# Packed attention and a SoLU layer on one core: v of three batches without zero rows, two banks for its weighted halves, a split last copy and a new order

## Chip, core and metric

The kernel runs on one core of a Trainium2 chip. Its engines work side by side: TensorE (PE in the profile) multiplies matrices, with the weight loads shown as PEld; VectorE (DVE), ScalarE (ACT) and GpSimd (POOL) work on vectors; SyncE (SP) issues the DMA transfers. Each engine executes its own list of instructions in order, and semaphores make one wait for another. The metric is the device time of the program in microseconds, and a change is judged by the median of several executions.

## The reference

Two stages follow each other. The first is attention over packed queries, for 8 batches of 8 heads with 576 tokens and 64 dimensions: 32 packed queries p look at all keys, and then all queries look at the 32 packed rows. The second is a layer over the 4608 tokens of 512 values, with 1024 hidden values and 64-bit weights.

```python
def sm_attn(qq, kk, vv):                      # scale = 1/8
    s = scale * np.matmul(qq, kk.transpose(0, 1, 3, 2))
    s = s - np.max(s, axis=-1, keepdims=True)
    a = np.exp(s)
    a = a / (np.sum(a, axis=-1, keepdims=True) + 1e-09)
    return np.matmul(a, vv)
p_packed = sm_attn(p, k, v)
out = sm_attn(q, p_packed, p_packed)          # -> x, (4608, 512)
...
h = x @ w_in
e = np.exp(h - np.max(h, axis=-1, keepdims=True))
solu = h * e / (np.sum(e, axis=-1, keepdims=True) + 1e-09)
mu = np.mean(solu, axis=-1, keepdims=True)
var = np.mean((solu - mu) ** 2, axis=-1, keepdims=True)
out = ((solu - mu) / np.sqrt(var + 1e-06) * g_ln) @ w_out
```

## The kernel before

The work is cut into named steps. A step carries a batch (`s10/3`), a tile of 128 tokens (`m1-12`, of 36) or the letter w for the weights (`wb0/w`). Functions register each step with what it needs and which buffers it takes and gives back; the long string `ORDER` lists all steps, and each engine gets its instructions in that order. A suffix names the engine of a step (`:v` VectorE, `:p` GpSimd, `:a` ScalarE) or the first PSUM bank that it writes (`:0` to `:7`, of eight). So an instruction that waits holds up all that stands behind it on its engine.

**Attention, batch b.** `lk0`, `lk1` (L411), `lq0`, `lq1` (L416) and `lv` (L420) load halves of k and q, and v. The packed scores come in two halves `s10`, `s11` (L436, TensorE, f32); `mx` takes their row maximum (L440, VectorE), `mb` the bias, `ex` the exponential on ScalarE, `ri` adds the small guard to the sums (L461 where GpSimd does it), `rs` inverts them (L465). For batches 0 to 2 `tp0` to `tp2` transpose the exponentials on TensorE (L474) and `tc0` to `tc2` copy them to `e1T` (L148); for later batches `eh`, `el`, `et`, `ea` do this with a transposing DMA. `av` (L504) weights v: 40 matmuls into one bank, both halves of the heads side by side. `pp` scales the result (L144 or L142), `pe` takes a peak, `pt` (L520), `pc`, `pk`, `un`, `uq` transpose it and find its scale (`unit`). Then the second attention: `sx0`, `sx1` (L538, TensorE), `sb` (L560), `sm` (L563), `su`, `se`, `ss` (L572), `si`, `sr` (L583), `sn` (L586), `at` (L627, a transpose), `ah` and `al` (L639): its weights as two f16 parts. Only batch 0 does these in two halves (`ss0`, `ss1`). For the layer, `z0`, `z1` (L604) multiply the packed rows with w_in, and `zh`, `zl` (L622) store the product as two f16 parts.

**Token tiles.** `m1` (L723) gives the hidden values h in two banks; `nm` (L729) is the row maximum, `nb` the bias, `bd` (L740 and L742) a bound and the row's scale `s_row`; `ex` (L747) the exponential, `u` (L752) the product e * s_row * h, and only with `u` are the banks of `m1` free again. `yh`, `yl` (L763) split it in f16 parts, `tr` (L767) transposes them by DMA into `yT`; `mu`, `sq` (L771), `ca` (L775 and L776) and `cr` (L781, L782) give the output's factor; `m2a`, `m2b` (L789) multiply with w_out, `ev` scales the result into the output buffer `o_sb` (L142 or L144), and `st` (L796) stores it. Tiles don't come in the order of their numbers: the last to be worked on is tile 31.

**Weights.** The 64-bit floats are read as pairs of 32-bit words and converted on the chip: `lw0` to `lw3` load w_in, `lW0` to `lW3` w_out (L167); `wa` (L182, ScalarE) and `wl` (L188 on VectorE, L142 on ScalarE) take upper words and last bits, `wm` joins them (L199, VectorE, the full width of 1024), `wp` sums squares on TensorE (L207). For w_in, `wb0` takes the peak (L211), `wb1` spreads it (L214) and `wb` makes a power of two, the scale that `un/0` needs; `zw`, `zy` make f16 parts `w_hi`, `w_lo` for later batches. For w_out, `pw0`, `pw1`, `pw` do the same (L291 to L299), `cs` sums columns (L316), `cv` scales the sum, `ct` centres (L323), and `ch` (L148), `cl` (L329) make the f16 parts `wch`, `wcl` that `m2` reads. `hw` are fillers: two matmuls on ones whose result nobody reads (L240).

Buffers: two each of k, q, v, of the output, of `yhl` and `yT`. Part of the weights is loaded into the buffers of k, q, v and z.

## Time and profile before

| | |
|---|---|
| time, median of 3 | 372.27 us (371.93 to 373.23) |
| the profiled execution | 372.9 us, its span 371.1 us |
| mean granted clock of TensorE | 0.991 |
| busy share: TensorE, weight loads | 96%, 45% |
| busy share: VectorE, ScalarE, GpSimd | 75%, 56%, 58% |
| moved by DMA | 70.57 MB, 190 GB/s in the mean |

The span runs from the first to the last instruction; 1.8 us of the execution lie around it. TensorE's busy share is 90% or more in 34 of the 40 equal slices of the span, and below 80% in the first four and the last. VectorE is busy for 80% or more in slices 3 to 8, where the weights are converted and the first tiles come, and less from there on. The DMA engines are full in slices 2 to 5 (422 to 425 GB/s). The profile names a group of instructions by line, engine and operation, with the tile it writes and those it reads; "busy" of TensorE is counted with pipelined matmuls, so that a row of 16 matmuls can be shorter than the sum of its parts.

### The profile page before, as it was taken

The page shows a single profiled execution, that of the slowest core. Times are in us where ns is not written, and L with a number is a line of the kernel's source. Part 1 is how long each engine was busy: PE and PEld are TensorE (multiplying, and loading weights), DVE is VectorE, ACT ScalarE, POOL GpSimd, SP SyncE. Part 2 cuts the span into 40 slices and gives each one's busy share as a digit, 9 for nine tenths or more (in the row PEclk, how much of TensorE's full clock was granted, in tenths as well). Part 3 has the DMA queues.
Part 4 walks back from the last instruction along what each step waited for, and adds up shares of the span by engine and source line. Part 5 has one row for each costly group of instructions (what it writes and reads, how often), then busy time and mean ns, then how long its engine had stood idle before and what let it go on. Part 6 is the DMA issues. An engine that isn't in the chain of part 4 may idle for free.

```text
span 371.1 us, 7650 instructions
## 1 busy us (share of the span) xinstructions
PE 354.9 (96%) x3027; PEld 165.9 (45%) x3027; DVE 278.9 (75%) x421; ACT 209.1 (56%) x357; POOL 214.7 (58%) x304
## 2 busy tenths in 40 slices
PE   6757998999999999999999999999999999999997
PEld 5323554344444444454445445444444444444443
DVE  2388899979898779688788998666795696751820
ACT  3559389876957477364454673362645344641341
POOL 1036769999987755298536573457733674256330
PEclk9898999999999999999999999999999999999999
DMA  7999993599698775959887655135546332351661
GB/s 284 425 422 419 425 382 68 126 266 284 229 191 325 227 171 157 153 150 258 156 212 171 198 115 124 44 97 150 148 115 164 92 113 59 113 141 54 148 170 58
DMA packets 99349, 70.57 MB, mean 190 GB/s; under 512 B 88048, under 2 KB 88048, under 8 KB 97776
## 3 DMA queue, kind: packets, MB, share of 16 engines
q1 hardware_dynamic: 99312, 70.07, 64.8%
q8 instruction: 24, 0.39, 0.4%
q14 instruction: 13, 0.11, 0.1%
HBM read 38.80 MB, written 9.44 MB: 130 GB/s over the span
## 4 chain that ended last, share of the span: by engine, by line
PE 83%; DVE 7%; DMA 6%; POOL 3%; issue 1%; ACT 0%; SPq 0%; POOLq 0%
PE pa L789 41%; PE ps L723 23%; PE ps L789 8%; DMA qT<-in_q_dram 4%; PE ps L604 3%; PE ps L538 2%; PE pa L316 1%; PE pa L504 1%; DMA zh<-in_moe_w_in_dram 1%; POOL wcl L329 1%; PE ps L436 1%; DVE u L752 1%; DVE zl L622 1%; DVE nm L729 1%; DVE yT L323 1%; POOL s L586 1%
## 5 line engine op out<-in xcount | busy, mean ns | idle before, releaser
L789 PE MATMUL pa<-wch,yT 128*128 128x512 f16 x480 | 149.5, 379 | 0.8 <-ACT yhl L148 0.8
L789 PEld LDWEIGHTS <-yT 128*128 128x128 f16 x864 | 83.2, 98 | 104.5 <-issue 4.8
L789 PE MATMUL pa<-wcl,yT 128*128 128x512 f16 x240 | 91.0, 379 | 0.0
L729 DVE TENSOR_REDUCE nm<-ps 128x1 f32<-128x1024 f32 x36 | 43.9, 1220 | 29.1 <-PE ps L723 28.9
L763 POOL TENSOR_TENSOR yhl<-u,yhl 128x1024 f16<-128x1024 f32 x23 | 51.2, 2227 | 21.2 <-ACT yhl L148 9.8
L747 ACT ACTIVATE e<-ps,bias,unit 128x1024 f32<-128x1024 f32 x36 | 43.3, 1202 | 35.4 <-DVE bias L144 28.5
L723 PE MATMUL ps<-zh,a2h 128*128 128x512 f16 (+1 forms) x160 | 54.8, 380 | 0.1
L752 DVE SCALAR_TENSOR_TENSOR u<-e,s_row,ps 128x1024 f32<-128x1024 f32 x36 | 45.6, 1267 | 12.2 <-ACT e L747 9.6
L723 PE MATMUL ps<-zh,a2l 128*128 128x512 f16 (+1 forms) x160 | 54.6, 379 | 0.0
L723 PE MATMUL ps<-zl,a2h 128*128 128x512 f16 (+1 forms) x160 | 54.6, 379 | 0.0
L771 ACT ACTIVATE e<-u,negmu 128x1024 f32<-128x1024 f32 x36 | 41.1, 1143 | 8.0 <-DVE negmu L144 7.8
L723 PEld LDWEIGHTS <-a2h 128*128 128x128 f16 (+1 forms) x320 | 27.7, 100 | 33.9 <-issue 3.1
L740 POOL TENSOR_SCALAR bound<-nm,unit 128x1 f32<-128x1 f32 x22 | 18.9, 859 | 27.1 <-DVE nm L729 27.0
L789 PE MATMUL ps<-wch,yT 128*128 128x512 f16 x96 | 30.2, 379 | 0.0
L142 ACT ACTIVATE o_sb<-pa,c_row 128x512 f32<-128x512 f32 x22 | 14.9, 684 | 25.9 <-POOL c_row L782 9.2
L148 ACT CAST yhl<-u 128x1024 f16<-128x1024 f32 x20 | 20.7, 1041 | 15.3 <-DVE u L752 13.0
L781 POOL TENSOR_SCALAR c_row<-sq,k_out,s_eps 128x1 f32<-128x1 f32 x36 | 14.8, 411 | 20.1 <-ACT e L771 19.4
L782 POOL TENSOR_TENSOR c_row<-c_row,neg_half 128x1 f32<-128x1 f32 x36 | 22.3, 619 | 3.0
L775 POOL TENSOR_SCALAR s_eps<-se,s_row 128x1 f32<-128x1 f32 x36 | 14.5, 402 | 15.3 <-ACT e L747 12.2
L723 PEld LDWEIGHTS <-a2l 128*128 128x128 f16 (+1 forms) x160 | 14.3, 100 | 16.8
L763 DVE TENSOR_TENSOR yhl<-u,yhl 128x1024 f16<-128x1024 f32 x13 | 17.6, 1354 | 2.3 <-ACT yhl L148 2.2
L789 PE MATMUL ps<-wcl,yT 128*128 128x512 f16 x48 | 18.2, 379 | 0.0
...
## 6 DMA issues: line engine op xcount, KB each, us to landing
...
```

What stands on the lines that cost most here:

```text
L142: nc.scalar.activation(out, in_, AF.Copy, scale=scale)
L148: nc.scalar.copy(out, in_)
L723: nc.tensor.matmul(h[rows, 512 * n:512 * n + 512], lhsT=lhsT, rhs=z[:, r, 512 * n:512 * n + 512], start=t == 0, stop=t == end)
L729: nc.vector.tensor_reduce(out=nm, in_=st['h'], axis=AX.X, op=ALU.max, negate=True)
L740: eng.tensor_scalar(out=bound, in0=st['nm'], scalar1=st['nm'], scalar2=st['unit'][:, 2:3], op0=ALU.mult, op1=ALU.max)
L747: nc.scalar.activation(st['e'], st['h'], AF.Exp, bias=st['bias'], scale=st['unit'][:, 1:2], accum_out=st['se'])
L752: nc.vector.scalar_tensor_tensor(out=st['u'], in0=st['e'], scalar=st['s_row'], in1=st['h'], op0=ALU.mult, op1=ALU.mult, accum_out=st['su'])
L763: engines[on(f'yl-{i}', 'v')].tensor_tensor(out=st['y'][:, 1], in0=st['u'], in1=st['y'][:, 0], op=ALU.subtract)
L771: nc.scalar.activation(st['e'], st['u'], AF.Square, bias=st['negmu'], accum_out=st['sq'])
L781: nc.gpsimd.tensor_scalar(out=c_row, in0=st['sq'], scalar1=k_out[:, 0:1], scalar2=s_eps, op0=ALU.mult, op1=ALU.add)
L782: nc.gpsimd.tensor_tensor(out=c_row, in0=c_row, in1=neg_half, op=ALU.pow)
L789: nc.tensor.matmul(st['po'], lhsT=st['yT'][:, a, c], rhs=w[:, c], start=c == 0 and t == 0, stop=c == NFC - 1 and t == 2)
```

## The change

Four things change.

- **v.** For batches 0 to 2 (`NARROW`) v is laid out as nine blocks of 128 rows instead of ten, without the 64 zero rows that filled up each half of the heads. `load_v` is shorter by a tenth there, and `av` uses 64 rows of the middle block for each half. The two halves go to a bank each, so that `av` takes a pair of banks for these batches; it still has 40 matmuls. The second half runs its blocks from the last to the first.
- **The last tile's scaled copy.** Where the tile's index is 35, `output` scales the left 256 columns on ScalarE and the right 256 on VectorE.
- **The order.** `ORDER` is another list throughout, with other engines for many steps. Ahead of the first token tile: `lw1` is loaded ahead of `lk1/1`, and `lw3` behind `lq1/0`; `wl0` and `wl2` go to GpSimd (from VectorE and ScalarE); `at0/0` stands behind `wb0`; fillers are `hw8`, `hw47`, `hw44`, `hw32`, `hw25`, `hw45`, `hw39`, `hw21`, where they were `hw1`, `hw25`, `hw9`, `hw10`, `hw29`, `hw2`. Later, `m1-3` stands ahead of `m1-2`, and `cl3` goes to GpSimd, `yl-3` to VectorE. Both lists end with tile 31.
- **The rest** of the steps is the same, but for the fillers: ten pairs of matmuls in all, where there were nine.

```diff
@@ -20,6 +20,7 @@
 Z_TOP = 14
 A_TOP = 15
 Z16 = 2
+NARROW = 3
 E16 = 3
 E_TOP = 15
 LIFT = 0.6931471805599453 * E_TOP
@@ -27,69 +28,69 @@
 Z_W = 2.0 ** 13
 W_HOME = 'zh zl zh zl kT qT v zh'.split()
 ORDER = '''
-lg/w hw1/w:6 lw0/w hw25/w:7 gx/w wa0/w wl0/w:v wm0/w lw2/w wa2/w wl2/w:a lk0/0 hw9/w:6 s10/0:0 mx0/0 lk1/0 s11/0:2
...
-sq-35 cr-35 ev-35:a ev-32:v st-32 hw33/w:7 hw27/w:7 st-35 hw31/w:7 ca-31 cr-31 ev-31:a st-31
+lg/w gx/w hw8/w:6 lw0/w wa0/w lw2/w wl2/w:p lk0/0 lk1/0 lk0/1 s10/0:0 s11/0:2 mx0/0 mb0/0:a ex0/0 mx1/0 mb1/0:v ex1/0
...
+ev-34:v st-34 hw2/w:7 mu-31:a hw26/w:7 sq-33 cr-33 ev-33:a sq-31 cr-31 ev-31:a st-33 zz/6 st-31
 '''
 
 @with_exitstack
@@ -417,7 +418,9 @@
 
         def load_v():
             st['v'] = raws.tile([P, H * HALF + H * J], F32, name='v', bufs=2)
-            nc.sync.dma_start(st['v'], v[b])
+            wide = H * HALF + H * J * (b >= NARROW)
+            at = b * H * HALF + max(0, b - NARROW) * H * J
+            nc.sync.dma_start(st['v'][:, :wide], v[:, at:at + wide])
 
         def banks(t):
             return (t[:, :512], t[:, 512:])
@@ -494,19 +497,25 @@
             st['e1T'] = att.tile([P, 2 * S], F32, name='e1T')
             by('ea', '').tensor_tensor(out=st['e1T'], in0=st['eT'][:, 0], in1=st['eT'][:, 1], op=ALU.add)
 
+        def halved(t):
+            return (t[:, :D], t[:, D:2 * D])
+
         def av():
-            pav = st['pav'] = one()
+            narrow = b < NARROW
+            st['pav'] = [x[:, :D] for x in banks(two())] if narrow else halved(one())
             e1T, v = (groups(st['e1T']), st['v'].rearrange('p (n g d) -> p n g d', g=G, d=D))
             odd = 2 * S // P // 2
             for r in range(2):
-                for x in range(odd + 1):
+                turn = [(odd * r + x, odd * r + x + r * (not narrow)) for x in range(odd + 1)]
+                for c, n in turn[::-1] if narrow and r else turn:
+                    rows = slice(LEFT * r, LEFT * r + LEFT) if narrow and c == odd else slice(0, P)
                     for g in range(G):
-                        nc.tensor.matmul(pav[32 * g:32 * g + 32, r * D:(r + 1) * D], lhsT=e1T[:, odd * r + x, 32 * g:32 * g + 32], rhs=v[:, (odd + 1) * r + x, g], start=x == 0, stop=x == odd)
+                        nc.tensor.matmul(st['pav'][r][32 * g:32 * g + 32], lhsT=e1T[rows, c, 32 * g:32 * g + 32], rhs=v[rows, n, g], start=c == (2 * odd if narrow and r else odd * r), stop=c == (odd if narrow or r == 0 else 2 * odd))
 
         def pp_rows():
             pp = st['pp'] = att.tile([P, 2, 2, D], F32, name='pp')
             for r in range(2):
-                src = st['pav'][:, r * D:(r + 1) * D].unsqueeze(1).broadcast_to([P, 2, D])
+                src = st['pav'][r].unsqueeze(1).broadcast_to([P, 2, D])
                 scaled(on(f'pp/{b}', 'v'), pp[:, r], src, st['rs'][:, r:r + 1])
 
         def row_peak():
@@ -658,7 +667,7 @@
             at('et', e_swap, after=['el'], takes='eT', gives='eh@eh')
             at('ea', e_join, after=['et'], takes='e1T', gives='eT@et')
         turned = [f'tc{i}' for i in range(3)] if b < E16 else ['ea']
-        at('av', av, after=turned + ['lv'], takes='bank', gives=f'e1T@{turned[0]} v@lv')
+        at('av', av, after=turned + ['lv'], takes='bank bank' if b < NARROW else 'bank', gives=f'e1T@{turned[0]} v@lv')
         at('pp', pp_rows, after=['av', 'rs'], takes='pp', gives='bank@av')
         at('pe', row_peak, after=['pp'])
         at('pt', pp_turn, after=['pp'], takes='bank')
@@ -790,7 +799,11 @@
 
         def output():
             st['o'] = mlp.tile([P, DM], F32, name='o_sb', bufs=2)
-            scaled(on(f'ev-{i}', 'a'), st['o'], st['po'], st['c'])
+            if i == B * S // P - 1:
+                for eng, cols in (('a', slice(0, DM // 2)), ('v', slice(DM // 2, DM))):
+                    scaled(eng, st['o'][:, cols], st['po'][:, cols], st['c'])
+            else:
+                scaled(on(f'ev-{i}', 'a'), st['o'], st['po'], st['c'])
 
         def store():
             nc.sync.dma_start(out[row:row + P, :], st['o'])
@@ -876,9 +889,11 @@
                 a = a.reshape(8, 128, 2304)
         elif name == 'v':
             a = a.reshape(8, 4, 2, 576, 64).transpose(0, 2, 3, 1, 4).reshape(8, 2, 576, 256)
-            a = _np.pad(a, ((0, 0), (0, 0), (0, 64), (0, 0)))
+            narrow = a[:NARROW].reshape(NARROW, 9, 128, 256)
+            a = _np.pad(a[NARROW:], ((0, 0), (0, 0), (0, 64), (0, 0)))
             a[:, 1] = _np.roll(a[:, 1], 64, axis=1)
-            a = a.reshape(8, 10, 128, 256).transpose(0, 2, 1, 3).reshape(8, 128, 2560)
+            a = a.reshape(8 - NARROW, 10, 128, 256)
+            a = _np.concatenate([x.transpose(1, 0, 2).reshape(128, -1) for x in [*narrow, *a]], axis=1)
         elif name == 'moe_g_ln':
             a = a.reshape(8, 128).transpose(1, 0)
         a = _np.ascontiguousarray(a)
```

SyncE, the first loads, from v of batch 0 on. Before (L411 loads k, L416 q, L420 v; `zl_206`, `zl_208`, `kT_210` are w_in's second and fourth quarter and w_out's first):

```order
L420 DMA v_181<-in_v_dram 128x2560
L411 DMA kT_179<-in_k_dram 128x1152
L416 DMA qT_195<-in_q_dram 128x1152 x2
L167 DMA zl_206<-in_moe_w_in_dram 128x2048
L167 DMA zl_208<-in_moe_w_in_dram 128x2048
L167 DMA kT_210<-in_moe_w_out_dram 128x2x1024
```

The same stretch after, where the lines count a little higher (`zl_176` and `zl_318` are now w_in's second and fourth quarter, `kT_142` is the second half of batch 1's k):

```order
L423 DMA v_174<-in_v_dram 128x2304
L168 DMA zl_176<-in_moe_w_in_dram 128x2048
L417 DMA qT_262<-in_q_dram 128x1152
L412 DMA kT_142<-in_k_dram 128x1152
L417 DMA qT_262<-in_q_dram 128x1152
L168 DMA zl_318<-in_moe_w_in_dram 128x2048
L168 DMA kT_322<-in_moe_w_out_dram 128x2x1024
```

v is narrower, a quarter of w_in has moved ahead of k's second half, and that half now stands between the halves of q.

VectorE, around the peak of the weights (`wb0`, L211). Before (L188 `wl3`, L199 `wm3`, L627 `at0/0`, L225 the first instruction of `wb`):

```order
L188 TENSOR_SCALAR u_372<-zl_208 128x1024
L583 RECIPROCAL sm_296<-sm_296 128x18
L199 SCALAR_TENSOR_TENSOR w_in_sb_82<-e_341,u_372 128x1024
L627 STREAM_TRANSPOSE s2_386<-s2_294 128x576
L211 TENSOR_REDUCE w_peak0_388<-pa0_79 128x1
L572 TENSOR_REDUCE sm_296<-s2_294 128x18
L225 TENSOR_REDUCE w_pow_96<-pa0_79 128x1
```

After (L189 `wl3` and, on `kT_322`, `wl4`; L212 `wb0`):

```order
L189 TENSOR_SCALAR u_356<-zl_318 128x1024
L581 TENSOR_REDUCE sm_279<-s2_277 128x18
L200 SCALAR_TENSOR_TENSOR w_in_sb_82<-e_360,u_356 128x1024
L189 TENSOR_SCALAR u_367<-kT_322 128x1024
L592 RECIPROCAL sm_279<-sm_279 128x18
L212 TENSOR_REDUCE w_peak0_383<-pa1_80 128x1
L581 TENSOR_REDUCE sm_279<-s2_277 128x18
L226 TENSOR_REDUCE w_pow_96<-pa1_80 128x1
```

The transpose `at0/0` is gone from between `wm3` and the peak; `wl4` and two small steps of batch 0 have come there.

GpSimd, at the first token tiles. Before (L740 and L742 are `bd` of tiles 1, 2 and 3, L461 is `ri/2`, L329 `cl1` and `cl2`, L763 `yl-1`):

```order
L740 TENSOR_SCALAR bound_632<-nm_573,unit_432 128x1
L742 TENSOR_SCALAR s_row_634<-bound_632 128x1
L461 TENSOR_SCALAR ssum_638<-es_576 128x2
L329 TENSOR_TENSOR wcl_84<-yhl_446,wch_83 128x1024
L740 TENSOR_SCALAR bound_665<-nm_661,unit_432 128x1
L742 TENSOR_SCALAR s_row_667<-bound_665 128x1
L329 TENSOR_TENSOR wcl_84<-yT_437,wch_83 128x1024
L740 TENSOR_SCALAR bound_707<-nm_684,unit_432 128x1
L742 TENSOR_SCALAR s_row_709<-bound_707 128x1
L763 TENSOR_TENSOR yhl_704<-u_669,yhl_704 128x1024
```

After (L749 and L751 are `bd` of tiles 1, 3 and 2, L784 and L785 `ca-1`, L330 `cl1`, L464 `ri/2`):

```order
L749 TENSOR_SCALAR bound_593<-nm_580,unit_432 128x1
L751 TENSOR_SCALAR s_row_595<-bound_593 128x1
L784 TENSOR_SCALAR s_eps_597<-se_591,s_row_595 128x1
L785 TENSOR_SCALAR s_eps_597<-s_eps_597,unit_432 128x1
L330 TENSOR_TENSOR wcl_84<-yhl_468,wch_83 128x1024
L749 TENSOR_SCALAR bound_690<-nm_667,unit_432 128x1
L751 TENSOR_SCALAR s_row_692<-bound_690 128x1
L464 TENSOR_SCALAR ssum_700<-es_574 128x2
L749 TENSOR_SCALAR bound_751<-nm_705,unit_432 128x1
L751 TENSOR_SCALAR s_row_753<-bound_751 128x1
```

The bounds of the three tiles have moved closer together: `ca-1` and `cl1` stand ahead of the second, `ri/2` ahead of the third, and `cl2` has moved behind them.

## Rows read from the trace of the kernel before

**Rows 1.** The page: busy time of each engine, share of the span, instructions.

```profile
PE 354.9 (96%) x3027; PEld 165.9 (45%) x3027; DVE 278.9 (75%) x421; ACT 209.1 (56%) x357; POOL 214.7 (58%) x304
```

**Rows 2.** Stages: window; length; PE, PEld, DVE, ACT, POOL busy (count); clock, DMA share, GB/s.

```profile
28.57:31.98 3.41, 1.18 (x17) 0.80 (x18) 2.36 (x4) 2.99 (x5) 1.91 (x1) 1.00 1.03 419
31.98:35.40 3.42, 3.42 (x33) 0.64 (x32) 3.14 (x14) 3.35 (x4) 2.01 (x2) 0.50 1.04 427
35.40:46.39 10.99, 10.99 (x92) 5.66 (x85) 9.48 (x17) 5.24 (x6) 8.62 (x7) 1.00 1.02 424
46.39:80.63 34.24, 32.43 (x432) 15.34 (x431) 32.22 (x49) 30.45 (x59) 29.73 (x32) 1.00 0.67 205
80.63:367.40 286.77, 286.75 (x2216) 131.32 (x2209) 217.22 (x316) 151.97 (x259) 168.23 (x250) 1.00 0.61 157
```

**Rows 3.** Chain of work that ended last: start (us), length (us), work.

```profile
6.16 15.99 DMA qT<-in_q_dram
...
28.25 2.24 POOL s L586
...
31.29 0.19 DVE w_peak L211
...
31.52 0.49 PE pa L214 x2
32.01 3.55 PE ps L604 x32
```

**Rows 4.** Timeline, TensorE, z of batch 1: start (us), length (us), work.

```profile
65.04 1.95 PE L604 MATMUL ps<-w_in_sb,ppT 64*32 64x512 f32 x32
```

**Rows 5.** Timeline, ScalarE, first use of w_in's last quarter, [idle before <- releaser].

```profile
27.04 1.17 ACT L182 ACTIVATE e<-zl 128x1024 f32<-128x1024 f32 x1 [0.61 <-DMA zl<-in_moe_w_in_dram]
```

**Rows 6.** Groups by line and form, VectorE, 0 to 80 us: busy, mean ns | idle.

```profile
L440 DVE TENSOR_REDUCE nmx<-ps 128x1 f32<-128x576 f32 x10 | 7.4, 746 | 4.6 <-PE ps L436 4.6
L199 DVE SCALAR_TENSOR_TENSOR w_in_sb<-e,u 128x1024 int32<-128x1024 int32 x4 | 5.2, 1296 | 0.6 <-ACT e L182 0.5
...
L323 DVE SCALAR_TENSOR_TENSOR yT<-yT,gs,o_sb 128x512 f32<-128x512 f32 x4 | 2.7, 748 | 0.0
...
L188 DVE TENSOR_SCALAR u<-zl 128x1024 int32<-128x1024 int32 x2 | 1.4, 688 | 0.0
```

**Rows 7.** Timelines, ScalarE from 36.98 us and TensorE at the last column sums.

```profile
36.98 1.16 ACT L142 ACTIVATE u<-zh 128x1024 int32<-128x1024 uint32 x1
...
38.05 1.15 ACT L182 ACTIVATE e<-zh 128x1024 f32<-128x1024 f32 x1
...
44.59 1.96 PE L316 MATMUL pa<-yhl,g_mean 128*128 128x512 f32 x4
```

**Rows 8.** Waits of TensorE: line <- releaser: us in total, times, longest.

```profile
PE pa L789 <- ACT yhl L148: 0.8, 1, 0.8
```

**Rows 9.** Chain of work that ended last, sx1/1 and a parted half.

```profile
79.57 1.13 PE ps L538 x32
...
98.69 2.59 PE pa L789 x12
...
101.28 0.65 PE ps L436 x16
101.93 2.70 PE pa L789 x12
```

**Rows 10.** Timeline, GpSimd: zw for w_hi, bd-1, bd-2 and cl2.

```profile
38.61 2.85 POOL L144 TENSOR_SCALAR w_hi<-w_in_sb,w_pow 128x1024 f16<-128x1024 f32 x1
...
51.30 1.98 POOL L740 TENSOR_SCALAR bound<-nm,unit 128x1 f32<-128x1 f32 x1 [3.18 <-DVE nm L729]
...
56.17 0.38 POOL L740 TENSOR_SCALAR bound<-nm,unit 128x1 f32<-128x1 f32 x1
...
56.78 2.14 POOL L329 TENSOR_TENSOR wcl<-yT,wch 128x1024 f16<-128x1024 f32 x1
```

**Rows 11.** Timeline, ScalarE, the last scaled copy.

```profile
367.46 0.69 ACT L142 ACTIVATE o_sb<-pa,c_row 128x512 f32<-128x512 f32 x1 [4.49 <-PE pa L789]
```

More of the change, by code (lines that the diff above doesn't have):

```diff
@@ L35 @@
-wm3/w wp3/w at0/0 wb0/w wb1/w tc2/1:a ss1/0 wb/w z0/0:4 z1/0:0 si1/0:p sr1/0 sn1/0:p wl4/w:a wa4/w wm4/w wa6/w wl6/w:a
-ri/1:p un/0 wm6/w ah0/0:a uq/0 wa5/w wl5/w:v wm5/w cs0/w:6 cs1/w wp4/w:7 lk0/2 cs4/w cs5/w cs2/w zh0/0:a zw3/w:p at1/0
-cs3/w lk1/2 wp5/w s10/2:2 zl0/0 wl7/w:a wp6/w wa7/w rs/1 zh1/0:a wm7/w mx0/2 ah1/0:a lv/1 wp7/w pw0/w al0/0:p al1/0:p
-s11/2:4 pw1/w zl1/0 lq0/1 lq1/1 pw/w mx1/2 cs6/w cs7/w cv/w:a mb0/2:a ko/w gd/w ct0/w ct1/w ct4/w mb1/2:a m1-1:0 ct5/w
-nm-1 ex0/2 av/1:7 m1-2:2 lk0/3 bd-1:p ct2/w ex1/2 ri/2:p ch0/w:a pp/1:a ct3/w ct6/w ch2/w:a nb-1:a ch1/w:a cl1/w:p ex-1
@@ new lines @@
+wa1/w pp/0:v pe/0 pt/0:6 hw44/w:7 mx0/1 lq0/0 pc/0:a sx0/0:0 lk1/1 hw32/w:7 sb0/0 lq1/0 sm0/0 mb0/1:v s11/1:2 mx1/1
+wp0/w:7 wl1/w:a hw25/w:0 ex0/1 sx1/0:4 lw3/w su0/0:p se0/0 lW0/w mb1/1:a ex1/1 tp0/1:1 wm1/w tp1/1:0 sb1/0 wp1/w sm1/0
+su1/0:p wp2/w tp2/1:2 wl3/w:v ss0/0 si0/0:p wa3/w hw45/w:3 wm3/w hw39/w:3 wl4/w:v wp3/w se1/0 sr0/0 hw21/w:3 wa4/w wb0/w
+pk/0 tc0/1:a ss1/0 tc1/1:a wb1/w sn0/0:p si1/0:a lW2/w wa6/w wb/w wm4/w zw0/w:p z0/0:4 z1/0:0 wl6/w:a ri/1:p lW1/w wa5/w
+un/0 wl5/w:a sr1/0 tc2/1:v zh1/0:a wp4/w:7 lW3/w wa7/w sn1/0:p cs0/w:6 wm6/w wl7/w:a cs1/w cs4/w zh0/0:a at0/0 ah0/0:a
```

112 lines of the change are left out of this document (56 added, 56 removed).

## The prediction, made before the changed kernel was run

> **What bounds the kernel now.** First the page: TensorE is busy for 96% of the span [rows 1]. Then the table of stages tells where the other 4% are [rows 2]. From 80.63 to 367.40 us TensorE is busy for 286.75 of 286.77 us, so nothing that saves time on another engine can shorten that stretch; only TensorE's own list can. Idle time is left in two places: before 35.40, where loads and the vector engines set the pace, and from 46.39 to 80.63, where TensorE is busy for 32.43 of 34.24 us (1.81 us idle) while VectorE is busy for 32.22. So a reader should ask two things: when may the first token tile (m1-1, at 46.39) start, and how much waits between it and m1-4 (at 80.63)? Behind m1-4 both kernels have the same TensorE steps left.
>
> The chain of waits gives the start [rows 3]. Batch 0's second half of q lands at 22.15. VectorE works on; then GpSimd's sn0/0 runs from 28.25 to 30.49, VectorE's at0/0 behind it, and only then come the peak of the weights (wb0, 31.29), wb1 on TensorE (31.52) and z0/0 at 32.01. z0 and z1 take 3.55 us, since the granted clock is 0.50, the lower of its two levels, from 31.98 to 35.40 [rows 2]; the same pair for batch 1 takes 1.95 us [rows 4].
>
> **The change, part by part.** The sum goes against the profiled execution: span 371.1 us, 1.8 us around it, 372.9 in all, 0.6 above the median of 372.27. I carry the difference over to the median.
>
> Loads. A narrow v is 128 rows of 256 words, 131 KB, shorter; at 419 to 427 GB/s [rows 2] that is 0.3 us a batch, and the DMA engines are full (share 1.02 to 1.04) while the weights come. In the new order lw1 stands ahead of lk1/1. Ahead of the landing of lk1/1 now lies what lay ahead of that of lq1/0, plus lw1 (1.05 MB), less a part of q (0.59) and the 0.13: 0.33 MB more, 0.8 us, so it lands at 22.95. lw3, last of w_in in both, has 0.13 MB less ahead of it: 26.7 instead of 27.04 [rows 5]. Later loads gain up to 0.9 us by v; from 46.39 on the DMA engines' share is down to 0.67, and the longest wait of TensorE there is for another engine [rows 8], so I cost that at nothing.
>
> VectorE to wb0. s11/1 follows at 23.0 and takes 0.65 (a half alone, [rows 9]). From 23.65 VectorE's list is mx1/1, sb1/0, sm1/0 and ss0/0 at 0.75, wm1 and wm3 at 1.30, wl3 and wl4 at 0.69, sr0/0 and wb0 at about 0.25 (durations of [rows 6]): 7.5 us, 31.1. Successive instructions overlap a little (four L323 of 748 ns fill 2.7 us), which makes it 30.4. I take 30.7. wb1 takes 0.49 [rows 3], so z0/0 starts at 31.2, 0.8 earlier: at0/0 and its wait for GpSimd now stand behind wb0.
>
> Clock. Between 28.57 and 31.98 TensorE was busy for 1.18 of 3.41 us [rows 2], and the clock fell right behind. Three fillers (hw45, hw39, hw21) now stand here, two matmuls each of 0.22 us (twelve of that width take 2.59, [rows 9]): 1.3 us more. I expect clock 1.00 and z done at 33.2, 2.3 earlier. Little of that can be used. TensorE has 10.99 us of work from there to m1-1 [rows 2], which would give 44.2; but wp7 needs wm7, and the last column sums stand behind the peak pw0. ScalarE has seven full-width steps from wa6 (its load lands at about 31.7) to wl7, 1.07 us start to start [rows 7]: 39.2. VectorE has fifteen steps from wb0 to pw0: four wm and two zl at 1.30, ss1 and two transposes at 0.75, and some 3.0 us of small ones (wb's seven, un, sr1, tc2, rs, pw0): 13.0 us, 12.2 with the overlap, so pw0 ends at 42.9 to 43.7. Then pw1 0.49, and cs6 and cs7 1.96 [rows 7]: m1-1 at 45.3 to 46.2. I take **45.5, a gain of 0.9**. At clock 0.50 z would end at 34.8 and m1-1 come at 45.8, so the clock is worth only 0.3 of it.
>
> wl0 and wl2 move to GpSimd. No row shows that operation there. The nearest are 2.14 (L329) and 2.85 us (a scaled copy of the same width, [rows 10]): from 8.6 both are done by 12.9 to 14.3. wm0, the first to want wl0, stands on VectorE behind mb1/0, and what it delays (tc1/0, av/0, pp/0) then waits for lk1/1 at 22.95 in any case. Nothing at either end.
>
> From m1-1 to m1-4. VectorE sets this stage. From ct0 to al/1, the last thing that m1-4 needs, its list is as long as before: one full-width step goes to GpSimd (cl3), one comes (yl-3), and a few small ones. It starts 1.0 earlier, with pw0. TensorE's waits change; before, the longest was 0.8 us, of m2a-3 for its transposed tile, which the view puts down to yh, the step that the tile is made by [rows 8]. Now av/2 waits for tc2/2, which stands behind five full-width ScalarE steps (1.07), six of half the width (about 0.65) and three small ones: some 10.5 us from cv at 45.5, where TensorE arrives at 55.9 (three token tiles at 2.59 and 2.6 us of small steps). 0 to 1 us, 0.5 taken. The narrow av takes two banks, so s11/3 waits for pp/2, and s10/3 for u-3; 0.4 together, and 0.3 more spread. **1.2 us instead of 1.8, a gain of 0.6.** One more pair of halves is parted (s10/4, then s11/4 with sx0/2, then sx1/2): a half alone costs 0.65 and 0.11 on the next f16 matmuls (2.70 for 2.59), a pair 1.13 [rows 9]: **0.3 lost**. av keeps its 40 matmuls a batch; eight read 64 rows, but s1 and sx read 64 rows too and go by their columns: nothing.
>
> Behind m1-4. Same steps; some pairs parted, others joined: within 0.1. Three close places come. m1-12 stands 3.7 us behind z1/2 and takes its bank, with sb0/3, zh1/2, mx1/5 and zl1/2 (4.1 us by the lengths above, the first begun earlier) between on VectorE. z1/6 needs av/7's bank 0.8 us behind it. m2a-28 follows its buffer's release by 4.1 us, where a transpose lands after 3.7. Each is met if VectorE is not late: 0 to 1 us together, nothing taken, since TensorE was idle for 0.02 us in that stretch before [rows 2].
>
> The end. The split copy is made where the tile's index is 35. But the last words of both orders are tile 31's: behind m2b-35 TensorE still has four halves (10.4 us). No one waits for tile 35's copy; tile 31's is still one ScalarE copy of 0.69 [rows 11]. Gain 0; a split of the right one might have given half of it, 0.3.
>
> Sum: -0.9 - 0.6 + 0.3 = -1.2. 372.27 - 1.2 = **371.1 us**.
>
> **Rivals.** More gain: the 6.16 MB from lw2 to lq1/0 took 16.0 us [rows 3], where 14.6 would do at 422 GB/s. What held that load may fall elsewhere. Then lk1/1 lands 1.4 earlier, wb0 moves to about 29.7, m1-1 to 44.6, and TensorE meets fewer waits: 369.8.
>
> The vector engines eat it (no change): clock 0.50 again, VectorE's durations laid end to end (m1-1 at 46.2), 1.5 us idle in the second stage: -0.2 - 0.3 + 0.3, or 372.1. For it speaks that VectorE is full there; against it, that its list is not longer.
>
> GpSimd holds the rows' scale back (slower): bd-1, ca-1, cl1, bd-3, ri/2 and bd-2 now stand in one row on GpSimd, and u-3 and u-2 wait for bd-3 and bd-2. In a quiet stretch bd's first instruction takes 0.38, but beside VectorE's ct steps it took 1.98 [rows 10]. At that price three times (2.3 with the second instruction), 0.8 for ca-1 and 2.1 for cl1, from 49.5, where nm-1 ends, bd-2 ends at 59.5, and with ri/2 as slow at 61.2; u-2 is wanted at 58.0. Each us behind 58.0 is a us for m1-0 and all that follows: +1.5 to +3.2, at 2.6 373.7. Against it: the ct steps end at about 52.7, before bd-3. The Trainium skill has a rule for such a row (SBUF — State Buffer, section Who interferes with whom): a VectorE instruction with two SBUF inputs and a GpSimd instruction that reads SBUF exclude each other for the whole instruction. The row of 1.98 agrees; by the rule each bd could lose a full VectorE step of 1.3, and u-2 would be late by 1 or 2.
>
> The change doesn't do what it says: that holds for the last tile, and is in the sum.
>
> **How the numbers follow.** A measurement of this kernel can tell about 0.3%, 1.1 us, from no change, so the line to faster is at 371.15, close to the forecast. Forecast (370.3 to 372.0): 0.48, of which 0.27 lie below the line. More gain: 0.18. No change: 0.17. Slower: 0.17. So faster 0.45, same 0.38, slower 0.17. The range runs from 369.4, 0.4 under the case of more gain, to 373.2, where the close places and part of GpSimd's lateness are in; about 0.05 and 0.13 lie outside.
>
> **What would show it.** z0/0 at 31.2 with clock 1.00 behind it; m1-1 at 45.5; m1-4 near 79.4, with TensorE idle for 1.2 us between; no idle time behind it; an end as long as before. Wrong, if m1-1 starts after 46, if bd-3 or bd-2 ends last before u, or if TensorE waits at m1-12, z1/6 or m2a-28.

## The result: slower by 1.2%, and the profile after

The changed kernel takes 376.62 us (median of 4, 376.15 to 377.14), the kernel before 372.1 in the same session: ratio 1.0116, 95% interval 1.0091 to 1.0141. Forecast were 371.1 (369.4 to 373.2). The profiled execution has a span of 375.0 us where the kernel before had 371.1.

The stages of the profiled execution of after, cut at the same steps as [rows 2]: up to z0/0, z, up to m1-1, up to m1-4, and then three pieces. Columns: window; length; busy time of PE, PEld, DVE, ACT, POOL (instructions); granted clock, DMA share, GB/s.

```profile
28.46:31.43 2.97, 1.44 (x14) 0.97 (x13) 2.97 (x6) 2.55 (x4) 2.02 (x3) 1.00 1.01 411
31.43:33.38 1.95, 1.95 (x33) 0.49 (x32) 1.78 (x8) 1.89 (x4) 1.10 (x2) 1.00 1.02 418
33.38:44.88 11.50, 10.92 (x85) 5.50 (x86) 10.93 (x26) 8.18 (x9) 8.81 (x9) 1.00 1.03 426
...
44.88:79.95 35.07, 33.89 (x432) 14.97 (x430) 31.87 (x50) 30.92 (x57) 27.58 (x31) 1.00 0.73 220
79.95:118.08 38.13, 38.13 (x379) 18.45 (x371) 35.22 (x50) 22.08 (x39) 30.40 (x36) 1.00 0.76 203
118.08:124.42 6.34, 3.76 (x11) 1.39 (x11) 1.22 (x1) 4.39 (x9) 5.95 (x9) 0.73 1.11 234
124.42:370.87 246.45, 246.43 (x1826) 111.60 (x1825) 185.65 (x270) 122.70 (x208) 132.67 (x205) 1.00 0.55 143
```

Read beside [rows 2], they hold the whole story. m1-1 starts at 44.88, 1.51 us earlier than before (46.39). From m1-1 to m1-4, with 432 matmul records in both kernels, it takes 35.07 us instead of 34.24: TensorE idles 0.63 less (1.18 for 1.81) but is busy for 1.46 more. So m1-4 comes 0.68 earlier. Then, from m1-4 to the last matmul, it takes 290.92 us instead of 286.37: 4.55 more, and nearly all of it lies in one short window, from 118.08 to 124.42. In the 246 us behind that TensorE is busy to 0.02 us.

The chain of work that ended last (start, length, work) shows the same three places; the rows answer to [rows 3].

```profile
6.42 16.58 DMA kT<-in_k_dram
...
30.72 0.24 DVE w_peak L212
...
45.04 2.59 PE ps L732 x12
...
108.55 2.50 POOL unit L346
...
113.21 2.09 POOL yhl L772
...
119.90 0.73 ACT e L457 x2
120.67 4.45 PE pa L798 x12
```

And this is TensorE's timeline at that window (start, length; in brackets the idle time before and what ended it). It stands still from 118.08 to 120.67, at m2a-6, which then takes 4.45 us where twelve such matmuls take 2.59 [rows 9]: the granted clock is 0.50 from 121.01 on, for 3.4 us.

```profile
120.67 0.39 PE L798 MATMUL pa<-wch,yT 128*128 128x512 f16 x1 [2.58 <-ACT e L457]
120.89 0.51 PE L798 MATMUL pa<-wcl,yT 128*128 128x512 f16 x1
```

The releaser named there is only the event that came last. Tile 6's transposition (tr-6) was issued at 115.32 (SyncE's timeline), and the view of its line gives 5.3 us to its landing, which is 120.62, and names the weight loads of m2a (PEld, L798) as what waited for it:

```profile
115.32 1.58 SPq L776 DMA_TRANSPOSE yT<-yhl  x1
...
who waited for it (us, times):
  PEld L798: 2.7, 1
...
DMA to landing us min/median/max: 5.3/5.3/5.3
```

That landing, not ScalarE's exponential, is what m2a-6 waits for. In the profiles of five variants below TensorE's timeline names the transfer itself.

So the sum of the profiled executions is: -1.51 at the start; -0.63 idle time and +1.46 busy time up to m1-4; +2.58 wait and +1.70 clock at m2a-6 (its eleven intervals from matmul to matmul take 4.07 us, where 0.216 each make 2.37); +0.27 behind, which was not followed further. Together +3.87, which is how much later the last matmul starts (370.87 for 367.00).

### The profile page after: what moved, and what is told of

Read it like the earlier page. It is cut to its first block, busy times and chain, and to the rows that moved or that the text cites. A ratio compares the mean times of both kernels' runs of the same rounds, so it can differ in the third digit from the quotient of the medians.

```text
span 375.0 us, 7664 instructions
## 1 busy us (share of the span) xinstructions
PE 358.2 (96%) x3029; PEld 165.6 (44%) x3029; DVE 282.6 (75%) x430; ACT 205.9 (55%) x348; POOL 218.3 (58%) x305
## 4 chain that ended last, share of the span: by engine, by line
PE 77%; DVE 9%; DMA 6%; POOL 3%; ACT 2%; issue 2%; SPq 0%; DVEq 0%; POOLq 0%
PE pa L798 35%; PE ps L732 22%; PE ps L798 8%; DMA kT<-in_k_dram 4%; PE ps L547 2%; PE ps L613 2%; PE pa L317 2%; PE ps L439 2%; DVE nm L738 2%; DMA zh<-in_moe_w_in_dram 1%; PE ps L513 1%; DVE u L761 1%; DVE mx L572 1%; DVE sm L581 1%; DVE w_in_sb L263 1%
## 5 line engine op out<-in xcount | busy, mean ns | idle before, releaser
L798 PE MATMUL pa<-wch,yT 128*128 128x512 f16 x464 | 146.1, 382 | 3.2 <-ACT e L457 2.6
L798 PEld LDWEIGHTS <-yT 128*128 128x128 f16 x864 | 83.4, 98 | 108.2 <-issue 7.3
L798 PE MATMUL pa<-wcl,yT 128*128 128x512 f16 x232 | 88.6, 382 | 0.0
L761 DVE SCALAR_TENSOR_TENSOR u<-e,s_row,ps 128x1024 f32<-128x1024 f32 x36 | 45.5, 1269 | 12.3 <-ACT e L756 9.0
L772 POOL TENSOR_TENSOR yhl<-u,yhl 128x1024 f16<-128x1024 f32 x19 | 41.3, 2177 | 14.2 <-DVE yhl L151 6.1
L749 POOL TENSOR_SCALAR bound<-nm,unit 128x1 f32<-128x1 f32 x22 | 15.9, 723 | 43.7 <-DVE nm L738 43.7
L790 POOL TENSOR_SCALAR c_row<-sq,k_out,s_eps 128x1 f32<-128x1 f32 x36 | 20.2, 562 | 25.5 <-ACT e L780 25.0
L798 PE MATMUL ps<-wch,yT 128*128 128x512 f16 x112 | 35.0, 379 | 0.0
L772 DVE TENSOR_TENSOR yhl<-u,yhl 128x1024 f16<-128x1024 f32 x17 | 21.7, 1276 | 2.5 <-ACT yhl L149 2.3
L443 DVE TENSOR_REDUCE nmx<-ps 128x1 f32<-128x576 f32 x16 | 12.0, 749 | 12.4 <-PE ps L439 12.4
L798 PE MATMUL ps<-wcl,yT 128*128 128x512 f16 x56 | 21.2, 379 | 0.0
```

What stands on the lines that cost most here:

```text
L749: eng.tensor_scalar(out=bound, in0=st['nm'], scalar1=st['nm'], scalar2=st['unit'][:, 2:3], op0=ALU.mult, op1=ALU.max)
L761: nc.vector.scalar_tensor_tensor(out=st['u'], in0=st['e'], scalar=st['s_row'], in1=st['h'], op0=ALU.mult, op1=ALU.mult, accum_out=st['su'])
L772: engines[on(f'yl-{i}', 'v')].tensor_tensor(out=st['y'][:, 1], in0=st['u'], in1=st['y'][:, 0], op=ALU.subtract)
L790: nc.gpsimd.tensor_scalar(out=c_row, in0=st['sq'], scalar1=k_out[:, 0:1], scalar2=s_eps, op0=ALU.mult, op1=ALU.add)
L798: nc.tensor.matmul(st['po'], lhsT=st['yT'][:, a, c], rhs=w[:, c], start=c == 0 and t == 0, stop=c == NFC - 1 and t == 2)
```

## The experiments

Theory A is that sum: one late tile (wait and clock, 4.3 us), av of the narrow batches (0.41 each), and an early start that is real. Each run is compared with the kernel before of its own session. In the lines of some variants the numbers of the code lines are 2 higher.

**One word: yl-6 on VectorE.** It takes tr-6 out of GpSimd's row.

```diff
-... at/2 yh-6:a yl-6:p tr-6 ex-5 ...
+... at/2 yh-6:a yl-6:v tr-6 ex-5 ...
```

> The changed kernel with one word of its order altered: yl-6 (the low half of tile 6) runs on VectorE instead of GpSimd. In the changed kernel's trace TensorE stands still from 118.08 to 120.67 us, at m2a-6, whose transposed tile lands at 120.62; it was issued at 115.32, right behind yl-6, which GpSimd ran at 113.17 to 115.30, behind sn/2, uq/2, bd-5 and bd-8. Then the granted clock is 0.50 from 121.01 to 124.42, where the twelve matmuls of m2a-6 take 4.45 us instead of 2.59. Theory A: this one late tile is 2.6 + 1.7 = 4.3 us of the 4.5 that the change costs. VectorE was free from 112.2 to 113.2, so the tile is issued by 114 and lands before 118.1; no idle time and clock 1.00 there: 376.6 - 4.3 = 372.3, between 371.8 and 373.0. Rival B: the new order is late at many places of GpSimd, and what is freed here comes back at the next one (u-5 and u-8 are late by a step of VectorE, or m2a-7 or m2a-8 wait): over 374.5.

Measured: 372.94 us against 372.1, ratio 1.0017 (1.0002 to 1.0032). One step of 1.2 us on another engine gives back 3.7 of the 4.5 us. In its profile tr-6 is issued at 112.6 and its tile lands 3.7 us later; TensorE waits 0.2 and 0.5 us in that stretch, for u, and the clock stays at 1.00. Rival B, a new order that is late everywhere on GpSimd, falls. What is left of the early start (m1-1 at 44.51 here) is still used up: from m1-4 to the last matmul it takes 287.68 us where the kernel before took 286.37, 0.74 of them idle (0.02 before) and 0.59 more of them busy.

**Fillers into the wait.** Six pairs of matmuls on ones ahead of m2a-6.

```diff
-... ex0/5 zh0/2:a m2a-6:7 ...
+... ex0/5 zh0/2:a hw0/w:7 hw1/w:7 hw3/w:7 hw4/w:7 hw5/w:7 hw6/w:7 m2a-6:7 ...
```

> The changed kernel with six more fillers (two matmuls on ones each, 0.43 us, so 2.6 us in all) on TensorE right ahead of m2a-6, where TensorE stood still from 118.08 to 120.67. Nothing else is moved. Theory A: the wait itself stays, since the transposed tile still lands at about 120.6, but TensorE is busy through it and the granted clock stays at 1.00 behind it: m2a-6 takes 2.6 us instead of 4.45, and the time is 376.6 - 1.8 = 374.8 (374.3 to 375.4). Rival C: the fall of the clock at 121.01 has nothing to do with the idle time before it: 376.6, clock 0.50 at the same place. If the fillers end later than the tile's landing, up to 0.4 of the gain is lost.

Measured: 376.4 us, ratio 1.0117 (1.0097 to 1.0136): the mechanism is there and the gain is not. The clock stays at 1.00 from 15.72 to 374.12 us and m2a-6 goes at full speed. But now m2a-28 waits:

```profile
313.01 0.39 PE L800 MATMUL pa<-wch,yT 128*128 128x512 f16 x1 [1.31 <-DMA yT<-yhl]
```

That one wait takes back 1.3 of the 1.7 us. Its tile landed 5.3 us behind its issue, where the same tile landed after 3.7 in the changed kernel. m2a-28 was one of the three close places of the prediction.

**Padded v in the new order.**

```diff
-NARROW = 3
+NARROW = 0
```

> The changed kernel with no narrow batch: v comes with its zero rows in all eight batches, 128 x 2560, and av uses one bank and whole blocks of 128 rows, as in the kernel before; the new order stays. In the changed kernel av of batches 0 to 2 takes 1.66 to 1.73 us where it took 1.25 to 1.32 before: between a matmul of 128 rows and one of 64 the next start comes 0.145 us after the last instead of 0.035, and that at three or four places of each av. Theory A: this costs 0.41 us a batch, of which batches 1 and 2 (0.8) lie on the path; av back at 1.25 to 1.32, lk1/1 0.3 us later (0.13 MB more ahead of it), the wait at m2a-6 as it is: 376.6 - 0.8 + 0.3 = 376.1 (375.6 to 376.6). Rival D, that the narrow v is worth its place (0.3 us or more at the start and nothing lost in av): 376.6 to 377.2.

Measured: 377.27 us, ratio 1.0129 (1.0093 to 1.0164), with runs at 376.14 and 376.15 and others at 378.38 and 379.99. The profiled execution is the longest: the granted clock fell at 22.76 and at 33.00, m1-1 came at 47.05, and it fell again behind the wait at m2a-6. So the time settles nothing between theory A and rival D. The rows do: av of batch 1 in this kernel, in the changed one, and in the next experiment, each from the timeline of its own profile (x80, since the profile has two records for each of the 40 f32 matmuls).

```profile
49.74 1.32 PE L513 MATMUL ps<-v,e1T 128*32 128x64 f32 x80
```

```profile
47.56 1.73 PE L513 MATMUL ps<-v,e1T 128*32 128x64 f32 x80
```

**The two 64-row blocks side by side.**

```diff
-                for c, n in turn[::-1] if narrow and r else turn:
+                for c, n in turn:
...
-... start=c == (2 * odd if narrow and r else odd * r), stop=c == (odd if narrow or r == 0 else 2 * odd))
+... start=c == odd * r, stop=c == odd * (r + 1))
```

> The changed kernel, with the second half's blocks of av in rising order for the narrow batches, so that the two blocks of 64 rows stand next to each other (128 rows, 64, 64, 128) instead of apart (128, 64, 128, 64); the two banks stay. If each change of the row count costs 0.11 us (theory A), one change less inside av and, where 128-row matmuls follow, the same at the end: three changes instead of up to four, or two where four were: av 0.1 to 0.2 us shorter a batch, 1.45 to 1.6 us, and if the two blocks run side by side another 0.03. The time falls by 0.2 to 0.4, 376.2 to 376.5. Rival E: the second bank, not the rows, makes av longer: av stays at 1.66 to 1.73 and the time at 376.6.

```profile
47.38 1.51 PE L513 MATMUL ps<-v,e1T 128*32 128x64 f32 x80
```

Measured: 376.21 us, ratio 1.0118 (1.0097 to 1.0139), and av at 1.51. With whole blocks (no change of the row count) it takes 1.32, with the two 64-row blocks next to each other (two changes, in and out) 1.51, with them apart (three) 1.73. The second bank is there in both of the longer ones, so rival E, by which av stays at 1.66 to 1.73, falls. The starts of single matmuls, in the records of these traces, show where the time goes: 0.149 us from the last of 128 rows to the first of 64 and 0.146 us back, where successive groups start 0.036 apart, and the second group behind a change starts 0.060 behind the first: 0.135 a change in all, three times 0.135 in the changed kernel. By that price the two changes of this variant cost 0.27; some 0.08 come back, since the groups of the two 64-row blocks start only 0.007 apart when these stand next to each other.

The step from av to the next one costs the same with whole blocks (0.150) as behind 64 rows (0.147). The price isn't one of rows alone: from m1 (128 columns of the array) to a whole av (32), with 128 rows in both, it is 0.309 us, where m1's own matmuls start 0.216 apart. The Trainium skill (TensorEngine Tiling (Array Packing), section Key Properties) says that a change of the array's tiling mode, not of the tile alone, drains TensorE; the trace agrees in so far as every change measured here has a price of more than 0.09 us, and the drain itself no view shows.

**The split copy, on the tile that is last.** The kernel before, split where `i == 31`.

```diff
-            scaled(on(f'ev-{i}', 'a'), st['o'], st['po'], st['c'])
+            if i == 31:
+                for eng, cols in (('a', slice(0, DM // 2)), ('v', slice(DM // 2, DM))):
+                    scaled(eng, st['o'][:, cols], st['po'][:, cols], st['c'])
+            else:
+                scaled(on(f'ev-{i}', 'a'), st['o'], st['po'], st['c'])
```

> The kernel before, with the split copy on the tile that is worked on last, tile 31: the left 256 columns on ScalarE and the right 256 on VectorE. In the trace of the kernel before that copy is one ScalarE instruction of 0.69 us behind the last matmul, and the store stands behind it. Theory A (the last copy is on the path that sets the end, and the change put the split on a tile in whose shadow 10.4 us of TensorE's work still lie): about half of 0.69, 0.3 us, is gained: 371.8 against 372.1 in the same session. Rival: the two halves wait for each other's bank or semaphore, and nothing is gained: 372.1.

Measured: 372.49 us against 372.47, ratio 1.0008 (0.9990 to 1.0027). The rival holds. ScalarE's half and then VectorE's half, from the timelines of this variant:

```profile
366.46 0.47 ACT L142 ACTIVATE o_sb<-pa,c_row 128x256 f32<-128x256 f32 x1 [4.49 <-PE pa L789]
```

```profile
366.97 0.48 DVE L144 TENSOR_SCALAR o_sb<-pa,c_row 128x256 f32<-128x256 f32 x1 [10.05 <-ACT o_sb L142]
```

VectorE waits for ScalarE: 0.47 and 0.48 us one behind the other, where one whole copy took 0.69 [rows 11]. From the last matmul's start to the store's issue it is 1.49 us instead of 1.18. In the changed kernel the halves of tile 35 stand in the same way (360.98 to 361.45 and 361.54 to 362.02), in the shadow of the four halves of m2 that follow. The Trainium skill (PSUM — Partial Sum Buffer, section PSUM bank collisions raise a hardware error) says that two engines on the same bank and quadrant collide even at different columns and with two reads, and that the compiler orders them; the trace agrees as far as the order goes.

**The start alone.** The 151 words of the new order ahead of m1-1, then the old order for all steps that are left. Three steps of the start change their banks to suit, and zw3 stands for zw0 there.

```diff
-... zw0/w:p z0/0:4 z1/0:0 ... s11/2:0 ... mb0/2:p cs6/w cs7/w pw/w m1-1:4 lv/2 cv/w:a mx1/2 ...
+... zw3/w:p z0/0:0 z1/0:4 ... s11/2:4 ... mb0/2:p cs6/w cs7/w pw/w lq1/1 mx1/2 cv/w:a ko/w gd/w ...
```

> The new order only up to the first token tile (loads, weights, batches 0 and 1, fillers), with padded v and one bank for av, and from m1-1 on the kernel before, word for word in its order (zw3 stays early on GpSimd, as before). Theory A: the start of the change is a real gain, which the rest of the new order gives away: m1-1 starts at about 45.0 instead of 46.4, TensorE's waits up to m1-4 are as before (1.8 us, perhaps 0.5 more, since lk0/2 and what follows do not move with it), and the time is 372.1 - 1.2 = 370.9 (370.5 to 371.6). Rival F: the start is bought by work put off, and m1-4 comes no earlier than before: 372.1 or more. Where TensorE's granted clock falls once more in the start (3.4 us at 0.50), up to 1.5 us of it go.

Measured: 372.29 us against 372.47, ratio 0.9999 (0.9980 to 1.0018). m1-1 starts at 44.89, as theory A wants, but the time is rival F's (372.1 or more). The last matmul starts at 366.21 instead of 367.00; TensorE idles 2.48 us between these two starts instead of 1.82, most of the rest at one tile that landed 4.5 us behind its issue. The step from 46.39 to 44.89 is also smaller in most executions than in the two that were profiled first: in the profile of the variant above, whose start is the old one, m1-1 comes at 45.58, because the clock fell at 24.00 and not at 31.98, and its last matmul starts at 365.99, ahead of this one's. So the start is worth some 0.7 to 1.5 us where it is made, and not measurably anything at the end.

**uq/2 behind yl-6 on GpSimd.**

```diff
-nb-5:v uq/2 mu-4:a sq-4 bd-5:p bd-8:p zy0/w ea/4:v at/2 yh-6:a yl-6:p tr-6
+nb-5:v mu-4:a sq-4 bd-5:p bd-8:p zy0/w ea/4:v at/2 yh-6:a yl-6:p uq/2 tr-6
```

> The changed kernel with the four small steps of uq/2 behind yl-6 on GpSimd instead of ahead of bd-5. In the changed kernel's trace the first of them took 2.50 us (108.55 to 111.05), while VectorE ran zy0 (108.29 to 109.69) and ea/4 (109.59 to 110.93), both with two inputs in SBUF; the same instruction of uq/3 took 0.26 with VectorE idle. Theory G: GpSimd's instruction is held for as long as VectorE runs such steps, whichever instruction it is: now the first of bd-5 takes about 2.4 us in that place, yl-6 starts only 0.8 us earlier (uq/2's three other instructions), and TensorE still stands still at m2a-6 for 0.2 to 1.8 us: 374 to 376. Rival H: it is uq/2's own first instruction that is slow there: bd-5 takes 0.4, yl-6 starts by 110, and the wait at m2a-6 is gone: 372.9.

Measured: 373.38 us, ratio 1.0017 (0.9999 to 1.0036). GpSimd's timeline, first in the changed kernel (L346 is the first instruction of uq/2, L749 bd-5), then here:

```profile
106.32 2.13 POOL L595 TENSOR_TENSOR s<-s,sm 128x1152 f32<-128x1152 f32 x1 [3.04 <-DVE sm L592]
108.55 2.50 POOL L346 TENSOR_SCALAR unit<-unit,w_pow 128x1 f32<-128x1 f32 x1
...
111.94 0.37 POOL L749 TENSOR_SCALAR bound<-nm,unit 128x1 f32<-128x1 f32 x1
```

```profile
108.25 2.74 POOL L749 TENSOR_SCALAR bound<-nm,unit 128x1 f32<-128x1 f32 x1
...
114.09 0.26 POOL L346 TENSOR_SCALAR unit<-unit,w_pow 128x1 f32<-128x1 f32 x1
```

Theory G's mechanism holds, its time (374 to 376) does not: whichever one-column instruction stands in that place takes 2.5 or 2.7 us, and the same instruction elsewhere 0.26 or 0.37. VectorE in the changed kernel in that time:

```profile
108.29 1.40 DVE L263 SCALAR_TENSOR_TENSOR w_in_sb<-w_in_sb,w_pow,w_hi 128x1024 f16<-128x1024 f32 x1
109.59 1.34 DVE L498 TENSOR_TENSOR e1T<-eT 128x1152 f32<-128x1152 f16 x1
```

Both have two inputs in SBUF. The rule of the Trainium skill that the prediction named (SBUF — State Buffer, section Who interferes with whom) is what happens here, for two VectorE steps on end. The variant with yl-6 on VectorE has a third such row: there bd-5 (111.18) took 1.46 us, up to the end of yl-6 (111.37 to 112.55), which has two inputs in SBUF as well. The time fell by more than G alone explains: tr-6 went out at 114.0 and landed 3.6 us later, not 5.3, and that needed a reason.

**No fillers ahead of z/0.**

```diff
-... wa3/w hw45/w:3 wm3/w hw39/w:3 ... sr0/0 hw21/w:3 wa4/w ...
+... wa3/w wm3/w ... sr0/0 wa4/w ...
```

> The changed kernel without the three fillers hw45, hw39 and hw21 (two matmuls of 0.22 us each) between 27 and 31.1 us. In the changed kernel z of batch 0 ran at clock 1.00 in 1.95 us, and m1-1 came at 44.88; in the kernel before, without fillers there, the clock fell at 31.98 and z took 3.55. Theory A: without them the clock falls before or within z/0, z takes 3.4 to 3.6, and m1-1 comes 0.3 to 0.9 us later (the seven full-width steps of ScalarE and VectorE's list up to pw0 hide the rest); the time 376.9 to 377.5. Rival I: the clock stays at 1.00 without them: z at 1.95 us and 376.6.

Measured: 376.31 us (two runs), ratio 1.0097 (1.0059 to 1.0135). At the start theory A holds in kind: the clock fell at 30.65, z took 3.05 us (3.4 to 3.6 expected), m1-1 came at 45.55, 0.67 later. The time does not show it, because in this execution the clock stayed at 1.00 behind the wait at m2a-6, which was 2.65 us here too. So the fall behind that wait is not certain: four of the five profiled executions that have the wait have the fall.

**The store behind tr-6 out of the way.** In the first five profiles with a late tr-6, the store of tile 4 followed it by 2.18 or 2.19 us.

```diff
-yh-8:v st-4 m2a-7:4 ... s10/5:0 lq0/4 un/3 ... rs/4 tr-8 pp/4:a
+yh-8:v m2a-7:4 ... s10/5:0 un/3 ... rs/4 tr-8 st-4 lq0/4 pp/4:a
```

> The changed kernel with two transfers, the store of tile 4 and the first half of q of batch 4, issued behind tr-8 instead of right behind tr-6; no engine's work is moved. In the changed kernel tr-6 was issued at 115.32 and its tile landed 5.3 us later, at 120.62, where most transposed tiles of the same trace take 3.6 to 3.8 us. In all five runs so far in which the store of tile 4 was issued 2.18 or 2.19 us behind tr-6 it landed 5.25 to 5.43 us later; where the store came 2.64 and 3.41 us behind (yl-6 on VectorE, uq/2 later) 3.63 and 3.68. Theory J: the store's issue in that moment makes the tile late by 1.6 us, and GpSimd's row (bd-5 and uq/2 held by VectorE's steps) the rest of the wait: now the tile lands at 119.0, TensorE waits 0.9 instead of 2.58 at m2a-6, and the time is 376.6 - 1.6 = 375.0, or 373.3 if the clock stays at 1.00 behind the shorter wait. Rival K: the transposed tile is late there whatever is issued behind it: 376.6, and the wait stays at 2.6.

Measured: 375.18 us (five executions, 374.87 to 376.77), ratio 1.0072 (1.0045 to 1.0099). That is the time of theory J, but its mechanism falls: in the profiled execution (376.23) nothing is issued behind tr-6 for 4.5 us, the tile still lands after 5.4, and TensorE waits 2.77 us. Why three of the executions took 374.9 to 375.2 is not shown; none of them was profiled. The DMA view from tr-6's issue (114.8) to its landing (120.3), 40 slices, busy share in tenths, and its queues:

```profile
DMA  0000000008999999999999900000000000500000
...
q1 hardware_dynamic: 2080, 0.52, 83.8%
q8 instruction: 1, 0.02, 1.0%
```

The tile's data are moved by 118.0. Then the engines stand all but idle for 1.5 us, move a little at 119.5, and the end is signalled at 120.2. One other packet is in that window, of an instruction queue, q8. Its records give 117.81 as its start.

**The packet out of the way.** Twenty tiny matmuls at 6 us, where TensorE stands still.

```diff
+        for i in range(20):
+            nc.tensor.matmul(pairs[i % 3][:32, ...], lhsT=ones_f[:, :32], rhs=ones_f[:, :32], start=True, stop=True)
```

> The changed kernel with twenty tiny matmuls more (32 x 32, 80 instructions of TensorE) right behind the warm-up, at about 6 us, where TensorE then stands still up to 10.6. Nothing behind it is altered. The page shows an instruction queue with 24 packets of 16 KB each; in the traces so far they come 256 TensorE instructions apart in the mean. In the ten profiled runs so far in which a transposed tile was issued with no other transfer in flight and one of these packets began 0.5 to 3.4 us behind its issue, 19 of 27 such tiles landed 4.6 to 5.6 us later; with none in that time 1 of 243 did (median 3.68). Theory L: it is this packet, which began at 118.51 in the changed kernel, that makes tr-6 (issued at 115.32) land at 120.62. With 80 instructions more ahead of it the packet comes when TensorE is 80 instructions less far, at about 112.5, before tr-6 is issued: tr-6 lands 3.6 to 3.8 us behind its issue, TensorE waits 0.9 us or less at m2a-6 instead of 2.58, and the time is 375.0, or 373.3 if the clock stays at 1.00 (other packets move as well, and may meet another tile: up to 0.7 back). Rival K: tr-6 is late by something else in that place: 5.2 to 5.4 us again, and 376.6.

Measured: 376.26 us, ratio 1.0117 (1.0082 to 1.0151). Theory L holds where it was put: the packet comes at 115.5, before tr-6's issue at 117.26, the store still follows by 2.19 us, the tile lands after 3.65, and m2a-6 waits 0.98, where 0.9 or less was expected:

```profile
120.95 0.39 PE L800 MATMUL pa<-wch,yT 128*128 128x512 f16 x1 [0.98 <-DMA yT<-yhl]
```

The clock stays at 1.00 behind it. The time of the profiled execution (376.46) is no better, since its start went badly: the clock fell at 22.68 and 32.92, and m1-1 came at 47.21, 2.3 us later than in the changed kernel; and m2a-28 waited 0.7. The other three (376.00 to 378.11) were not profiled, so for them it stays open. The packet is not the whole reason either: in the variant with uq/2 behind yl-6 one began 3.17 us behind tr-6's issue, as near as in the changed kernel (3.19), and the tile landed after 3.63. The expectation says ten profiled runs for its count; they were thirteen.

**Two ways back.** First the start alone, with the changed kernel's code for v and a narrow v for batch 0:

```diff
-NARROW = 3
+NARROW = 1
```

> The start-only version (the new order up to m1-1, the old one behind it) with a narrow v for batch 0 alone, whose av lies in the time in which TensorE waits for lk1/1 in any case; the last copy is whole. Theory A: what the narrow v is worth is its load, 0.13 MB less ahead of lk1/1: 0.3 us less, and av/0's 0.41 more costs nothing there: lk1/1 lands at 22.7 instead of 23.0, m1-1 starts 0.3 earlier, and the time is 0.3 us under the start-only version, 372.0 against 372.3 and 372.3 to 372.5 for the kernel before. Rival: m1-1 is set by ScalarE's and VectorE's lists behind the weights' loads, or what is gained is waited for again at m2a-11 (0.6 us there in the start-only version): no difference.

Measured: 371.89 us against 372.72, ratio 0.9982 (0.9966 to 0.9999): the only version here whose interval lies under the kernel before, by 0.7 us in its middle and by next to nothing at its edge. With twelve variants run, one such may be chance. The start-only version's ratio was 0.9999, so the difference of the two lies within their intervals, and in its profile m1-1 starts at 44.97, no earlier; what the narrow load gave is not shown.

Then the changed kernel with yl-6 on VectorE, `NARROW = 1` and no split copy:

> The changed kernel with three things undone or mended: yl-6 on VectorE, v narrow for batch 0 alone (batches 1 and 2 padded, one bank), and no split copy. If the costs add up (theory A): 372.9 with yl-6 on VectorE, less 0.82 for two av at 1.32 instead of 1.73, nothing for the copy, which was in the shadow of four halves of m2: 372.1, the time of the kernel before. So the changed kernel would be the kernel before, plus 3.7 for the late tile and the clock behind it, plus 0.8 for av; and its earlier start (1.5 us by the profiled executions) would be used up by parted halves and by later waits. Rival: the costs overlap, av's 0.8 being hidden behind waits that follow: 372.6 to 372.9.

Measured: 372.63 us against 372.72, ratio 1.0002 (0.9988 to 1.0015). The time of the kernel before is reached, and against yl-6 alone (1.0017, 1.0002 to 1.0032) 0.0015 or 0.6 us is won, with intervals that overlap. The profile says why not 0.82: around av/1 TensorE is 0.41 shorter, but the piece with av/2, from tp1/2 to m1-0, keeps its 4.60 us, because s11/3 and m1-0 then wait 0.12 and 0.15 for u. Theory and rival each have a part of this one.

## Why the prediction was wrong

**The start: right in kind, too small.** Forecast: lk1/1 at 22.95, z0/0 at 31.2 with clock 1.00 behind it, m1-1 at 45.5. Measured: 23.00, 31.43 and 1.00, 44.88. The step mis-sized is VectorE's list from wb0 to pw0, taken at 12.2 to 13.0 us: it took 11.7 (30.67 to 42.36). So it no longer set m1-1; TensorE, which had no gap from 33.96 on, came to pw1 only at 42.61 by its own list. The clock was worth 0.67 (no fillers), forecast 0.3.

**From m1-1 to m1-4: right in idle time, wrong in busy time.** Idle 1.18 us, forecast 1.2. But TensorE was busy for 1.46 us more, forecast 0.3. The first failed step is the sentence that av keeps its 40 matmuls, that s1 and sx read 64 rows too, "nothing". The same paragraph took 0.11 us for a half step alone from [rows 9] without asking what the 0.11 was. It fits the price of a change of a matmul's shape, there between 128 rows and columns and 64 rows and 32 columns. A narrow av makes three more changes, of the rows, 0.41 us, twice on the path (0.82). The rest is 0.64: by the two timelines the halves of sx take 0.34 more, those of m2 0.28 and z 0.23, and small steps 0.2 less. That this is the price of the parted halves was not tried apart.

**Behind m1-4: wrong, and this decided.** The failed step is "0 to 1 us together, nothing taken, since TensorE was idle for 0.02 us in that stretch before". It took the old order's clean record for the new order's. "Same steps; some pairs parted, others joined: within 0.1" was too small as well: with yl-6 on VectorE, so without the late tile, TensorE is still busy for 0.59 us more in that stretch and idle for 0.74. Three places were named as close; the one that broke, m2a-6, was none of them. There tr-6 stands behind sn/2, uq/2, bd-5, bd-8 and yl-6 on GpSimd, VectorE's zy0 and ea/4 hold the row up by 2.2 us (2.50 for 0.26), and a packet of an instruction queue goes with 1.6 us (5.3 for 3.7). Without the packet TensorE would have waited some 0.9 us (0.98 in the variant that moves it); without the hold some 0.3 (120.62 less 2.24, against 118.08), an estimate by the same numbers. The fall of the clock behind the wait costs the other 1.70.

**The rivals.** The slower one had the mechanism (GpSimd's one-column steps held by VectorE, a tile's step late behind them) and a time of 373.7, at chance 0.17; its place, bd-2 ahead of u-2, was wrong: bd-1 took 1.98 us again, but bd-2 was done at 57.1 and u-2, at 58.15, waited for ScalarE. The prediction looked for that mechanism only where GpSimd's list had visibly thickened, not in the 290 us behind.

**The end: right.** The split is in the shadow. That a split of tile 31 might have given 0.3 was wrong: it costs 0.3 in the path there, since the halves go one behind the other.
